# Splitting weights on ScalarE and VectorE instead of GpSimd, in a kernel of windowed attention and a GELU MLP

## The chip, the cores and the metric

The kernel runs on one core of a Trainium2 chip. The metric is the device time of one execution in microseconds (us). The engines of a core work side by side, each from its own queue in a fixed order: TensorE (PE: matrix products; PEld is its loading of stationary operands), VectorE (DVE), ScalarE (ACT), GpSimd (POOL) and SyncE (SP), which here issues DMAs. An instruction waits on semaphores for the instructions of other engines whose results or buffers it needs, and all that stands behind it in its engine's queue waits too.

## The reference

Eight batches of attention with 8 heads, 576 positions and head size 64, with a window of 128 positions back and a linear bias; the result, 4608 rows of 512, goes through an MLP with an exact GELU. All is float32.

```python
scores = scale * np.matmul(q, k.transpose(0, 1, 3, 2))
mask = (rel >= 0) & (rel < window)
scores = np.where(mask, scores + bias[None], -1000000000.0)
attn = np.exp(scores - np.max(scores, axis=-1, keepdims=True))
attn = attn / (np.sum(attn, axis=-1, keepdims=True) + 1e-09)
x = np.matmul(attn, v)            # transposed to 4608 x 512
h = x @ w_in                      # 512 x 2048, held as float64
g = 0.5 * h * (1.0 + erf(h * inv_sqrt2))
return g @ w_out                  # 2048 x 512, held as float64
```

## The kernel before

**Numbers in halves.** Most products are made in float16: an operand is scaled by a power of two, its float16 rounding is the high half, what is left is the low half, and three products (high by high, high by low, low by high) are summed. The high half is one pass of ScalarE or GpSimd, the low half one scalar_tensor_tensor of VectorE (`low_part`, line 148: in * scale - high). The scale needs the largest magnitude of the tensor: a maximum along the free axis (`absmax`, line 204), then one over the partitions (`over_partitions`, from line 109). The latter is done in one of two ways: with `early` by GpSimd's partition_all_reduce (line 113) and a floor on VectorE (114), otherwise by 13 small VectorE instructions (four copies of quarters, a reduction, a transpose, a reduction, a spread, a transpose, and four more; lines 118 to 129). `pow2` (131) and `inverse` (143) take the power of two out of the maximum by bit operations. Batches 0 to 2 use the early way (`b < 3` in `stat_v` and `split_qk`).

**Weights.** Each of w_in and w_out comes in 8 chunks of 128 x 1024 float64 words, seen as pairs of int32. `to_float32` (from line 179) makes float32 of a chunk: ScalarE takes the magnitude of the high word, read as a float (185); VectorE clamps it to two thresholds (186), shifts and masks (187), and puts in the sign and top bit (188) and three bits of the low word (191). `absmax` then finds the chunk's maximum. `split_weights` (from 195) makes the halves: ScalarE scales z in place (199) and rounds it (200), GpSimd subtracts (201). For w_in the chunks are zi, their halves wi; for w_out zo and wo. The first token tile multiplies with zo itself in float32; the later ones with wo.

**Buffers.** The raw chunks and the float32 chunks share a few slots (RAW_TAGS, Z_TAGS) with other tiles, so that a chunk can be loaded only when an earlier tenant of its slot has been read. zi 6 and 7 use the slot of zi 0 and 1 (tag ld), so ScalarE's pass on them waits until the halves of 0 and 1 are made.

**Attention.** A unit is a batch and a pair of heads: `scores` (sc, line 387, with the bias added by VectorE at 409 from the second batch on), `softmax` (maximum nmax, exponentials s on ScalarE at 450, high halves e on GpSimd at 459, or on ScalarE in batch 0, low halves on VectorE), two DMA transposes (et), and `weigh` (av, line 497), whose result ScalarE and VectorE split into x. A batch has 576 rows and a token tile 512, so that the end of a batch (tail, in batch 0) belongs to the next tile.

**MLP.** For a tile of 512 tokens, `mlp_in` (h, line 541: 16 blocks of 12 matmuls) and `mlp_out` (o, lines 576 and 579). For the first tile g is float32. For the others ScalarE makes GELU in float32 (557), GpSimd the high half (558), VectorE the low half. The product h has four PSUM banks (tag mm), shared with o; scores and av have four others (tag att).

**Order.** The program first runs batch 0's attention with w_in's conversion in between, then h of the first tile with w_out's conversion and batch 1's q, k, v, then o of the first tile with batch 1's attention and w_out's split; from then on, tile t's MLP with batch t+1's attention. The order in each queue is made by a scheduler before the run, from the program's order and priorities, and is fixed.

Of the kernel before, what the change touches and what calls it, by code (L numbers as in the profile page):

```python
# [52 lines left out]
def attention_gelu_mlp(  # L53
# [54 lines left out]

    def over_partitions(stat, n, early=False):


        if early:
            nc.gpsimd.partition_all_reduce(stat, stat, P, bass_isa.ReduceOp.max)
            nc.vector.tensor_scalar_max(stat, stat, FLOOR)
            return
# [62 lines left out]

    def to_float32(n, z):


        raw = raws.pop(n)
        lo, hi = raw[:, :, 0], raw[:, :, 1]
        zi = z.bitcast(I32)
        nc.scalar.activation(z, hi.bitcast(F32), AF.Abs)
        nc.vector.tensor_scalar(z, z, hi_thr, lo_thr, op0=ALU.min, op1=ALU.max)
        nc.vector.tensor_scalar(zi, zi, 3, 0x3FFFFFFF, op0=ALU.logical_shift_left, op1=ALU.bitwise_and)
        nc.vector.scalar_tensor_tensor(
            out=zi, in0=hi, scalar=-0x40000000, in1=zi, op0=ALU.bitwise_and, op1=ALU.bitwise_or
        )  # L190
        nc.vector.scalar_tensor_tensor(
            out=zi, in0=lo, scalar=29, in1=zi, op0=ALU.logical_shift_right, op1=ALU.bitwise_or
        )

    def split_weights(z, both, scale):

        hi = both[:, 0].rearrange("p c f -> p (c f)")
        lo = both[:, 1].rearrange("p c f -> p (c f)")
        nc.scalar.activation(z, z, AF.Copy, scale=scale)
        nc.scalar.copy(hi, z)  # L200
        nc.gpsimd.tensor_tensor(out=lo, in0=z, in1=hi, op=ALU.subtract)

# [5 lines left out]
    sww = pool.tile([P, NWP], F32, name="sww")  # L208
    pwo = pool.tile([P, NWP], F32, name="pwo")

    def weights_in(ns):

        zs = {}
        stat = small([P, len(ns)], f"stw{ns[0]}", 1)
        for n in ns:
            if n % 2 == 0:
                tag, bufs = Z_TAGS[n // 2]
                zz = pool.tile([P, 2, NW], F32, tag=tag, name=f"zi{n}", bufs=bufs)
            zs[n] = zz[:, n % 2]
            to_float32(n, zs[n])  # L220
            absmax(stat[:, n - ns[0] : n - ns[0] + 1], zs[n])
        over_partitions(stat, len(ns), True)
        r = slice(ns[0], ns[-1] + 1)
        nc.vector.tensor_scalar(pww[:, r].bitcast(I32), stat.bitcast(I32), EXPMASK, None, op0=ALU.bitwise_and)
        inverse(sww[:, r], pww[:, r])
        for n in ns:
            both = pool.tile([P, 2, NCC, 256], F16, name=f"wi{n}")
            split_weights(zs[n], both, sww[:, n : n + 1])
            wi.append(both)

    def weights_out_raw(m):

        if m % 2 == 0:
            zo.append(pool.tile([P, 2, NW], F32, tag="wo", name=f"zo{m}", bufs=4))
            zo.append(zo[m])
        to_float32(NWP + m, zo[m][:, m % 2])

    def weights_out_scale():


        for m in range(NWP):
            absmax(pwo[:, m : m + 1], zo[m][:, m % 2])
        over_partitions(pwo, NWP, True)
        nc.vector.tensor_tensor(out=pwo, in0=pwo, in1=pww, op=ALU.mult)
# [508 lines left out]
```

## Time and profile before

| what | before |
|---|---|
| median of 3 runs | 1025.76 us (1025.10 to 1026.47) |
| the profiled execution | 1023.53 us, of which span 1021.7 us |
| mean granted TensorE clock | 0.943 |
| TensorE, VectorE, ScalarE, GpSimd busy | 922.4, 653.3, 456.2, 293.9 us |
| HBM read, written | 47.32, 9.44 MB |

The span runs from the first to the last instruction of the trace. Rows of a timeline give start, duration, engine, line, operation, output<-input, count, and in square brackets the idle time ahead of it with what ended it. Rows of groups give busy time, the mean duration in ns of one, and the idle time just before them with its releasers. The parts of it that matter here are shown where they are used.

### The profile page before, as it was taken

The numbers are of one execution on the slowest core, as the hardware profiler recorded it, in microseconds if no ns is written. First come the engines' busy times: TensorE is split into PE (matmuls) and PEld (weight loads), VectorE is DVE, ScalarE is ACT, GpSimd is POOL, SyncE is SP. The second block draws the span as 40 slices with busy tenths as digits, with TensorE's granted clock in tenths as the row PEclk, the third lists the DMA queues.
The fourth block names the chain that finished last, engine by engine and source line by source line (L and its number), as shares of the span: only waits on it lengthen the run. The fifth ranks groups of instructions, "written<-read, shape, count | busy, mean of one in ns | idle before, by whom it ended". The sixth has DMA issues, their size and how long they took to land.

```text
span 1021.7 us, 17546 instructions
## 1 busy us (share of the span) xinstructions
PE 922.4 (90%) x6996; PEld 445.6 (44%) x6996; DVE 653.3 (64%) x1238; ACT 456.2 (45%) x971; POOL 293.9 (29%) x534
## 2 busy tenths in 40 slices
PE   5624998796597998999999999999999999999998
PEld 2322443343244544444445444544544444444443
DVE  5996968775397768776877787688746751201210
ACT  3755535544354446435644564356526722201200
POOL 0015020652243325411631253044314421200200
PEclk7658898797798999999999999999999999999999
DMA  9978341256124742462255234623322260000000
GB/s 286 231 170 239 110 175 66 47 114 161 47 94 83 180 110 48 93 171 63 47 104 161 62 73 89 165 66 68 84 59 47 47 125 11 1 21 21 1 11 31
DMA packets 192146, 96.69 MB, mean 95 GB/s; under 512 B 151360, under 2 KB 172864, under 8 KB 191936
## 3 DMA queue, kind: packets, MB, share of 16 engines
q1 hardware_dynamic: 187840, 87.18, 35.9%
q10 hardware_dynamic: 4224, 8.39, 2.4%
q8 instruction: 55, 0.90, 0.4%
q14 instruction: 27, 0.22, 0.1%
HBM read 47.32 MB, written 9.44 MB: 56 GB/s over the span
## 4 chain that ended last, share of the span: by engine, by line
PE 63%; DVE 17%; DMA 5%; issue 5%; ACT 5%; POOL 2%; SPq 2%; DVEq 0%; POOLq 0%; ACTq 0%
PE o L579 31%; PE h L541 21%; PE av L497 4%; PE sc L387 4%; DMA et<-e_main 3%; DMA v<-vp 2%; PE o L576 2%; DVE e_main L148 2%; DVE g L148 1%; DVE stv L204 1%; ACT s L450 1%; POOL g L558 1%; DVE stq L204 1%; SPq L293 1%; DVE stw L204 1%
## 5 line engine op out<-in xcount | busy, mean ns | idle before, releaser
L541 PE MATMUL h<-x,wi 128*128 128x512 f16 x1728 | 390.6, 385 | 24.6 <-ACT g L557 13.8
L541 PEld LDWEIGHTS <-wi 128*128 128x128 f16 x1728 | 168.0, 99 | 231.8 <-issue 37.0
L579 PE MATMUL o<-wo,g 128*128 128x512 f16 x1152 | 260.4, 380 | 3.3 <-DVE g L148 1.9
L579 PEld LDWEIGHTS <-g 128*128 128x128 f16 x1536 | 146.0, 98 | 179.2 <-DVE g L148 2.9
L558 POOL TENSOR_SCALAR g<-g,sg 128x512 f16<-128x512 f32 x128 | 106.6, 836 | 284.3 <-ACT g L557 274.7
L148 DVE SCALAR_TENSOR_TENSOR g<-g,sg,g 128x512 f16<-128x512 f32 x128 | 105.2, 834 | 95.8 <-POOL g L558 95.7
L450 ACT ACTIVATE s<-s,nmax 128x192 f32<-128x192 f32 x252 | 111.2, 442 | 102.9 <-DVE nmax L445 98.1
L557 ACT ACTIVATE g<-h,gs 128x512 f32<-128x512 f32 x128 | 86.0, 687 | 149.7 <-PE h L541 104.4
L459 POOL TENSOR_SCALAR e_main<-s,z 128x192 f16<-128x192 f32 x252 | 119.4, 492 | 109.6 <-ACT s L450 38.1
L148 DVE SCALAR_TENSOR_TENSOR e_main<-s,z,e_main 128x192 f16<-128x192 f32 x270 | 124.7, 504 | 21.4 <-POOL e_main L459 20.8
L497 PE MATMUL av<-et,vbuf 128*64 128x128 f16 (+1 forms) x1896 | 58.8, 227 | 45.3 <-DVE e L148 17.1
L387 PE MATMUL sc<-kbuf,qbuf 64*64 64x192 f16 (+1 forms) x1656 | 78.0, 273 | 22.2 <-DMA kbuf<-kp 9.3
L579 PE MATMUL o<-wo_first,g 128*128 128x512 f16 x384 | 88.9, 381 | 0.0
L497 PEld LDWEIGHTS <-vbuf 128*64 128x64 f16 x1896 | 55.1, 123 | 57.2 <-issue 36.0
L510 ACT ACTIVATE x<-av,cx 128x448 f16<-128x448 f32 (+7 forms) x56 | 26.7, 492 | 106.3 <-PE av L497 106.1
L409 DVE SCALAR_TENSOR_TENSOR s<-sc,cs,bias_h 128x384 f32<-128x384 f32 x112 | 63.8, 607 | 12.1 <-PE sc L387 11.9
L576 PE MATMUL o<-zo,g 128*128 128x512 f32 x128 | 61.1, 634 | 0.0
L445 DVE TENSOR_REDUCE nmax<-s 128x5 f32<-128x960 f32 (+1 forms) x56 | 58.6, 1046 | 3.1 <-POOL s L414 0.9
L414 POOL MEMSET s<- 64x128 f32 (+1 forms) x112 | 19.0, 171 | 136.2 <-DVE s L409 135.9
L387 PEld LDWEIGHTS <-qbuf 64*64 64x64 f16 x1512 | 37.9, 109 | 45.7 <-issue 41.7
L148 DVE SCALAR_TENSOR_TENSOR x<-av,cx,x 128x448 f16<-128x448 f32 (+7 forms) x56 | 27.9, 512 | 41.5 <-ACT x L510 41.2
L587 ACT ACTIVATE ob<-o,so 128x512 f32<-128x512 f32 x16 | 10.9, 679 | 90.3 <-PE o L579 90.2
(118 smaller groups left out, 708.0 us busy)
## 6 DMA issues: line engine op xcount, KB each, us to landing
v<-vp SPq DMA_DIRECT2D x32, 320.0 KB, 4.9
out<-ob SPq DMA_DIRECT2D x36, 256.0 KB, 2.1
raw<-w_in ACTq DMA_DIRECT2D x8, 1024.0 KB, 9.1
raw<-w_out SPq DMA_DIRECT2D x8, 1024.0 KB, 6.3
q<-qp SPq DMA_DIRECT2D x7, 1152.0 KB, 5.8
k<-kp SPq DMA_DIRECT2D x7, 1152.0 KB, 6.4
qbuf<-qp SPq DMA_DIRECT2D x4, 288.0 KB, 4.6
kbuf<-kp SPq DMA_DIRECT2D x4, 288.0 KB, 4.7
```

What stands on the lines that cost most here:

```text
L148: nc.vector.scalar_tensor_tensor(out=dst, in0=src, scalar=scale, in1=high, op0=ALU.mult, op1=ALU.subtract)
L387: nc.tensor.matmul(ps[bank][o, n, 0:W], a, m, start=(i == 0), stop=(i == len(terms) - 1 and b > 0), skip_group_check=True,)
L409: nc.vector.scalar_tensor_tensor(out=s[:, bank[0] : bank[0] + k, :], in0=ps[bank][:, 0:k, 0:W], scalar=cs, in1=bias.broadcast_to([P, k, W] ...
L445: nc.vector.tensor_reduce(out=nmax[:, r], in_=s[:, r], axis=AX.X, op=ALU.max, negate=True)
L450: nc.scalar.activation(s[:, i, :], src, AF.Exp, bias=nmax[:, i : i + 1], scale=scale, accum_out=z[:, i : i + 1])
L459: nc.gpsimd.tensor_scalar(e[:, i, 0, c], s[:, i], z[:, i : i + 1], 1.0, op0=ALU.mult, op1=ALU.mult)
L497: nc.tensor.matmul(av[r, (j - blocks[0]) * QB : (j - blocks[0] + len(js)) * QB], vbuf[:, vi, hp, kb, r], bass.AP(tensor=base.tensor, offse ...
L541: nc.tensor.matmul(ph, wi[n][:, a, cc, k * P : (k + 1) * P], x[:, cc, b, :], start=(i == 0), stop=(i == 3 * NCC - 1),)
L557: nc.scalar.activation(g32, ph, AF.Gelu, scale=gsc[t, n])
L558: nc.gpsimd.tensor_scalar(g[:, r, 0], g32, gsg[t, n], 1.0, op0=ALU.mult, op1=ALU.mult)
L576: nc.tensor.matmul(o, g[:, r, c], zo[n][:, n % 2, k * DM : (k + 1) * DM], start=(fc == 0), stop=(fc == NFC - 1))
L579: nc.tensor.matmul(o, g[:, r, a, c], wo[n][:, b, k, :], start=(fc == 0 and i == 0), stop=(fc == NFC - 1 and i == 2),)
```

## The change

It does four things. (1) `split_weights` makes the high half in one ScalarE pass, scaling and rounding at once, and the low half with `low_part` on VectorE; GpSimd has no part in it. (2) ScalarE's pass on the high words scales them by 2^-112, the upper threshold with it; the lower threshold goes, the mask after the shift goes, and the mask of the sign keeps one bit instead of two. (3) The clamp gives out its maximum over the chunk (`accum_out`), so that `absmax` on the weights goes; the maximum is now taken of words before the shift, so that its floor is another (STAT_FLOOR) and its power of two is made by a shift and a mask (`pow2_of_words`). (4) The third batch's scales for q, k and v are made by the 13 VectorE instructions (`b < 2`).

```diff
-    def over_partitions(stat, n, early=False):
+    def over_partitions(stat, n, early=False, floor=FLOOR):
         if early:
             nc.gpsimd.partition_all_reduce(stat, stat, P, bass_isa.ReduceOp.max)
-            nc.vector.tensor_scalar_max(stat, stat, FLOOR)
+            nc.vector.tensor_scalar_max(stat, stat, floor)
...
-    lo_thr = 2.0 ** -15 * 1.125
-    hi_thr = 122848.0
+    SQUEEZE = 2.0 ** -112
+    hi_thr = 122848.0 * SQUEEZE
+    STAT_FLOOR = 2.0 ** ((127 - 50) // 8 - 127) * (1 + (127 - 50) % 8 / 8)
...
-    def to_float32(n, z):
+    def to_float32(n, z, stat):
-        nc.scalar.activation(z, hi.bitcast(F32), AF.Abs)
-        nc.vector.tensor_scalar(z, z, hi_thr, lo_thr, op0=ALU.min, op1=ALU.max)
-        nc.vector.tensor_scalar(zi, zi, 3, 0x3FFFFFFF, op0=ALU.logical_shift_left, op1=ALU.bitwise_and)
+        nc.scalar.activation(z, hi.bitcast(F32), AF.Abs, scale=SQUEEZE)
+        nc.vector.tensor_scalar(z, z, hi_thr, None, op0=ALU.min, op1=ALU.max, accum_out=stat)
+        nc.vector.tensor_scalar(zi, zi, 3, None, op0=ALU.logical_shift_left)
         nc.vector.scalar_tensor_tensor(
-            out=zi, in0=hi, scalar=-0x40000000, in1=zi, op0=ALU.bitwise_and, op1=ALU.bitwise_or
+            out=zi, in0=hi, scalar=-0x80000000, in1=zi, op0=ALU.bitwise_and, op1=ALU.bitwise_or
         )
...
-        nc.scalar.activation(z, z, AF.Copy, scale=scale)
-        nc.scalar.copy(hi, z)
-        nc.gpsimd.tensor_tensor(out=lo, in0=z, in1=hi, op=ALU.subtract)
+        nc.scalar.activation(hi, z, AF.Copy, scale=scale)
+        low_part(lo, z, scale, hi)
+
+    def pow2_of_words(dst, stat):
+        nc.vector.tensor_scalar(
+            dst.bitcast(I32), stat.bitcast(I32), 3, EXPMASK, op0=ALU.logical_shift_left, op1=ALU.bitwise_and
+        )
...
-            to_float32(n, zs[n])
-            absmax(stat[:, n - ns[0] : n - ns[0] + 1], zs[n])
-        over_partitions(stat, len(ns), True)
+            to_float32(n, zs[n], stat[:, n - ns[0] : n - ns[0] + 1])
+        over_partitions(stat, len(ns), True, STAT_FLOOR)
...
-        for m in range(NWP):
-            absmax(pwo[:, m : m + 1], zo[m][:, m % 2])
-        over_partitions(pwo, NWP, True)
+        over_partitions(stwo, NWP, True, STAT_FLOOR)
+        pow2_of_words(pwo, stwo)
...
-        pwv[b], scv[b] = pow2(f"v{b}", stat, 1, 3, b < 3)
+        pwv[b], scv[b] = pow2(f"v{b}", stat, 1, 3, b < 2)
...
-        pw, sc = pow2(f"q{b}", stat, 2, 2, b < 3)
+        pw, sc = pow2(f"q{b}", stat, 2, 2, b < 2)
```

The scheduler makes another order of it. First place: GpSimd during the weights' conversion, before (stw, stv, stq are maxima of weights, v, q and k; ISA without operands is code that is put ahead of another kind of instruction):

```order
L113 ISA stw_764<-stw_764 128x2
L201 ISA
L201 TENSOR_TENSOR wi_463<-zi_446,wi_463 128x1024
...
L201 TENSOR_TENSOR wi_786<-zi_765,wi_786 128x1024
L113 ISA
L113 ISA stv_974<-stv_974 128x1
L113 ISA stw_790<-stw_790 128x2
L201 ISA
L201 TENSOR_TENSOR wi_808<-zi_791,wi_808 128x1024
L201 TENSOR_TENSOR wi_812<-zi_791,wi_812 128x1024
L113 ISA
L113 ISA stv_1088<-stv_1088 128x1
```

The same place now, up to the first e_main of batch 1 (s_0 are its scores, stwo the maxima of w_out):

```order
L113 ISA stw_757<-stw_757 128x2
L113 ISA stw_779<-stw_779 128x2
L113 ISA stv_959<-stv_959 128x1
L113 ISA stq_975<-stq_975 128x2
L422 MEMSET s_0_1200 64x128 x2
L422 MEMSET s_0_1200 64x64
L113 ISA stwo<-stwo 128x8
L467 ISA
L467 TENSOR_SCALAR e_main<-s_0_1200,z_0_1270 128x192 x5
```

The subtractions are gone with the ISA rows between them and the all-reduces; one ISA row is left, between w_out's all-reduce and batch 1's first high halves.

Second place: VectorE ahead of the last x of the first tile (x<-av_3_0, the low half that the first tile's h waits for), before:

```order
L148 SCALAR_TENSOR_TENSOR e_3_569<-s_3_471,z_3_568,e_3_569 128x192 x4
L114 TENSOR_SCALAR stw_764<-stw_764 128x2
L148 SCALAR_TENSOR_TENSOR x_379<-av_2_0_645,cx_0_249,x_379 128x512
...
L186 TENSOR_SCALAR zi_791<-zi_791 128x1024
L187 TENSOR_SCALAR zi_791<-zi_791 128x1024
L186 TENSOR_SCALAR zi_791<-zi_791 128x1024
L188 SCALAR_TENSOR_TENSOR zi_791<-raw_613,zi_791 128x1024
...
L204 TENSOR_REDUCE stv_974<-v_1_820 128x1
L191 SCALAR_TENSOR_TENSOR zi_791<-raw_613,zi_791 128x1024
L186 TENSOR_SCALAR zo_856<-zo_856 128x1024
...
L148 SCALAR_TENSOR_TENSOR x_379<-av_3_0_704,cx_0_249,x_379 128x512
```

And now:

```order
L148 SCALAR_TENSOR_TENSOR x_380<-av_2_0_638,cx_0_250,x_380 128x512
L148 SCALAR_TENSOR_TENSOR e_3_566<-s_3_468,z_3_565,e_3_566 128x192 x5
L190 TENSOR_SCALAR zi_780,stw_779<-zi_780 128x1024
L148 SCALAR_TENSOR_TENSOR e_3_566<-s_3_468,z_3_565,e_3_566 128x192 x4
...
L190 TENSOR_SCALAR zo_841,stwo<-zo_841 128x1024
L148 SCALAR_TENSOR_TENSOR wi_773<-zi_758,sww,wi_773 128x1024
L213 TENSOR_REDUCE stq_975<-q_1_886 128x1
L148 SCALAR_TENSOR_TENSOR wi_776<-zi_758,sww,wi_776 128x1024
...
L208 TENSOR_SCALAR pww<-stw_779 128x2
L148 SCALAR_TENSOR_TENSOR x_380<-av_3_0_697,cx_0_250,x_380 128x512
```

The weights' low halves (wi) stand between the last e_3 and the last x, the clamps have a second output, and the e_3 rows have moved behind x<-av_2_0.

Third place: ScalarE between batch 1's last x and the second tile's first GELUs (g_1), before:

```order
L510 ACTIVATE x_1510<-av_3_2_1997,cx_2_1100 128x128
L557 ACT_TABLE_LOAD
L557 ACTIVATE g_1_0_2072<-h_0_2058,gs_0_2052 128x512
...
L557 ACTIVATE g_1_5_2276<-h_5_2263,gs_0_2052 128x512
L344 ACTIVATE qbuf<-q_2_2033,scq_2044 128x2304
L344 ACTIVATE kbuf<-k_2_2034,scq_2044 128x2304
L557 ACTIVATE g_1_6_2293<-h_6_2280,gs_0_2052 128x512
```

And now:

```order
L518 ACTIVATE x_1504<-av_3_2_1985,cx_2_1101 128x128
L352 ACTIVATE qbuf<-q_2_2019,scq_2046 128x2304
L352 ACTIVATE kbuf<-k_2_2020,scq_2046 128x2304
L565 ACT_TABLE_LOAD
L565 ACTIVATE g_1_0_2074<-h_0_2060,gs_0_2054 128x512
L565 ACTIVATE g_1_1_2091<-h_1_2078,gs_0_2054 128x512
```

The third batch's q and k are split ahead of the first GELU instead of behind the sixth. On GpSimd, an ISA row, the all-reduce of their maxima and another ISA row stood between the first two high halves g of this tile; now nothing does.

More of the change, by code (lines that the diff above doesn't have):

```diff
@@ L157, in attention_gelu_mlp @@
     Z_TAGS = [("ld", 2), ("ld", 2), ("x", 2), ("ld", 2)]
-    lo_thr = 2.0 ** -15 * 1.125
-    hi_thr = 122848.0
+    SQUEEZE = 2.0 ** -112
+    hi_thr = 122848.0 * SQUEEZE
+    STAT_FLOOR = 2.0 ** ((127 - 50) // 8 - 127) * (1 + (127 - 50) % 8 / 8)
+    assert FLOOR == 2.0 ** -50
     NW = NCC * 256
@@ L209, in attention_gelu_mlp @@
     pwo = pool.tile([P, NWP], F32, name="pwo")
+    stwo = pool.tile([P, NWP], F32, name="stwo")
     def weights_in(ns):
@@ L219, in weights_in @@
             zs[n] = zz[:, n % 2]
-            to_float32(n, zs[n])
-            absmax(stat[:, n - ns[0] : n - ns[0] + 1], zs[n])
-        over_partitions(stat, len(ns), True)
+            to_float32(n, zs[n], stat[:, n - ns[0] : n - ns[0] + 1])
+        over_partitions(stat, len(ns), True, STAT_FLOOR)
         r = slice(ns[0], ns[-1] + 1)
-        nc.vector.tensor_scalar(pww[:, r].bitcast(I32), stat.bitcast(I32), EXPMASK, None, op0=ALU.bitwise_and)
+        pow2_of_words(pww[:, r], stat)
         inverse(sww[:, r], pww[:, r])
@@ L235, in weights_out_raw @@
             zo.append(zo[m])
-        to_float32(NWP + m, zo[m][:, m % 2])
+        to_float32(NWP + m, zo[m][:, m % 2], stwo[:, m : m + 1])
     def weights_out_scale():
-        for m in range(NWP):
-            absmax(pwo[:, m : m + 1], zo[m][:, m % 2])
-        over_partitions(pwo, NWP, True)
+        over_partitions(stwo, NWP, True, STAT_FLOOR)
+        pow2_of_words(pwo, stwo)
         nc.vector.tensor_tensor(out=pwo, in0=pwo, in1=pww, op=ALU.mult)
```

## The prediction, made before the changed kernel was timed

> **What bounds the kernel now.** I read the page's 40 slices first, then busy time by stretches, then the timeline of each engine where TensorE has gaps.
>
> ```profile
> PE 922.4 (90%) x6996; PEld 445.6 (44%) x6996; DVE 653.3 (64%) x1238; ACT 456.2 (45%) x971; POOL 293.9 (29%) x534
> ...
> PE   5624998796597998999999999999999999999998
> ...
> DVE  5996968775397768776877787688746751201210
> ...
> PEclk7658898797798999999999999999999999999999
> ```
>
> From slice 17 (about 410 us) on TensorE is full at full clock: nothing that the change touches can shorten that part, only move it. The 1021.7 - 922.4 = 99 us in which TensorE is idle, and the lower clocks, lie before it. Second view, stretches of 25 us (TensorE, its weight loads, VectorE, ScalarE, GpSimd busy; clock; DMA):
>
> ```profile
> 75.00:100.00 25.00, 13.08 (x113) 7.21 (x110) 15.04 (x11) 15.95 (x18) 13.90 (x6) 0.83 0.92 257
> 250.00:275.00 25.00, 12.73 (x54) 5.51 (x54) 9.08 (x12) 5.98 (x8) 7.24 (x7) 0.79 0.19 52
> 300.00:325.00 25.00, 19.89 (x183) 10.48 (x181) 19.07 (x59) 14.41 (x30) 9.80 (x21) 0.86 0.42 85
> ```
>
> In 75 to 100 and in 250 to 275 no engine is busy even two thirds of the time: something waits that is no work. GpSimd's own timeline says what:
>
> ```profile
> 80.50 13.90 POOL L201 TENSOR_TENSOR wi<-zi,wi 128x1024 f16<-128x1024 f32 x6 [7.08 <-ACT zi L199]
> 102.09 0.38 POOL L113 PARTITION_ALL_REDUCE stv<-stv  x1 [7.69 <-DVE zi L188]
> 140.31 0.38 POOL L113 PARTITION_ALL_REDUCE stv<-stv  x1 [8.06 <-issue]
> ...
> 251.71 2.56 POOL L558 TENSOR_SCALAR g<-g,sg 128x512 f16<-128x512 f32 x1 [14.17 <-ACT g L557]
> 262.19 0.37 POOL L113 PARTITION_ALL_REDUCE stq<-stq  x1 [7.92 <-issue]
> 270.06 2.46 POOL L558 TENSOR_SCALAR g<-g,sg 128x512 f16<-128x512 f32 x3 [7.51 <-issue]
> ```
>
> Each time GpSimd goes from arithmetic to PARTITION_ALL_REDUCE or back, 7 to 8 us pass with nothing running; the order shows a bare ISA row there. I call it a **swap**. Between 254.3 and 270.1 there are two, 7.92 + 7.51 = 15.4 us, between the first and the second half (g) that GpSimd makes of the second MLP tile's GELU.
>
> The Trainium skill, page "GPSIMD Engine Reference", section "2.1 Instruction dispatch", says that the first call of freshly loaded code pays a load of about 6 us. By that the two would be 12 us and term 4 below 3 us smaller; the rows show 7.5 to 8, and I go by them.
>
> VectorE and TensorE in the first MLP tile:
>
> ```profile
> 25.97 2.88 DVE L148 SCALAR_TENSOR_TENSOR vbuf<-v,scv,vbuf 128x2560 f16<-128x2560 f32 x1 [0.26 <-ACT vbuf L317]
> 72.79 1.40 DVE L148 SCALAR_TENSOR_TENSOR e<-s,z,e 128x192 f16<-128x192 f32 x4
> 76.50 0.75 DVE L148 SCALAR_TENSOR_TENSOR x<-av,cx,x 128x512 f16<-128x512 f32 x1 [2.23 <-ACT x L510]
> 85.92 1.44 DVE L186 TENSOR_SCALAR zi<-zi 128x1024 f32<-128x1024 f32 x1 [8.39 <-ACT zi L185]
> 92.34 3.14 DVE L188 SCALAR_TENSOR_TENSOR zi<-raw,zi 128x1024 int32<-128x1024 int32 x1
> 101.61 0.74 DVE L148 SCALAR_TENSOR_TENSOR x<-av,cx,x 128x512 f16<-128x512 f32 x1
> 140.72 0.15 DVE L114 TENSOR_SCALAR stv<-stv 128x1 f32<-128x1 f32 x1 [5.02 <-POOL stv L113]
> 167.72 1.22 DVE L204 TENSOR_REDUCE pwo<-zo 128x1 f32<-128x1024 f32 x1
> ```
>
> ```profile
> 82.89 4.32 PE L541 MATMUL h<-x,wi 128*128 128x512 f16 x18
> 90.46 4.98 PE L541 MATMUL h<-x,wi 128*128 128x512 f16 x15 [2.94 <-ACT x L510]
> 102.40 27.20 PE L541 MATMUL h<-x,wi 128*128 128x512 f16 x114 [6.96 <-DVE x L148]
> 139.93 22.48 PE L576 MATMUL o<-zo,g 128*128 128x512 f32 x52
> 166.60 1.92 PE L387 MATMUL sc<-kbuf,qbuf 64*64 64x192 f16 x30 [3.22 <-DVE kbuf L148]
> 186.55 1.17 PE L387 MATMUL sc<-kbuf,qbuf 64*64 64x192 f16 x12 [3.28 <-DVE s L409]
> 191.84 1.17 PE L387 MATMUL sc<-kbuf,qbuf 64*64 64x192 f16 x12 [2.11 <-DVE s L409]
> 192.93 16.41 PE L576 MATMUL o<-zo,g 128*128 128x512 f32 x34
> 234.68 2.77 PE L497 MATMUL av<-et,vbuf 128*64 128x128 f16 x66 [6.54 <-DMA et<-e_main]
> 251.66 10.52 PE L541 MATMUL h<-x,wi 128*128 128x512 f16 x48 [1.74 <-ACT g L557]
> 272.79 6.61 PE L541 MATMUL h<-x,wi 128*128 128x512 f16 x18 [10.61 <-ACT g L557]
> ```
>
> VectorE sets the pace of the first 140 us; TensorE waits for it and, through it, for GpSimd: 8.39 at 85.92 (ScalarE's pass into a buffer that GpSimd had not read yet, behind its swap of 7.08) and 5.02 at 140.72 (the second batch's maxima behind the swap of 8.06).
>
> **The change part by part.** Prices of one instruction:
>
> ```profile
> L201 POOL TENSOR_TENSOR wi<-zi,wi 128x1024 f16<-128x1024 f32 x8 | 18.7, 2363 | 21.7 <-ACT wi L200 14.6 <-ACT zi L199 7.1
> L204 DVE TENSOR_REDUCE stw<-zi 128x1 f32<-128x1024 f32 x8 | 9.7, 1216 | 0.0
> L191 DVE SCALAR_TENSOR_TENSOR zo<-raw,zo 128x1024 int32<-128x1024 int32 x8 | 9.8, 1222 | 0.0
> L185 ACT ACTIVATE zo<-raw 128x1024 f32<-128x1024 f32 x8 | 9.1, 1143 | 24.1 <-DMA raw<-w_out 24.1
> L199 ACT ACTIVATE zi<-zi,sww 128x1024 f32<-128x1024 f32 x8 | 8.6, 1140 | 0.0
> L186 DVE TENSOR_SCALAR zo<-zo 128x1024 f32<-128x1024 f32 x8 | 5.5, 684 | 0.0
> L129 DVE TENSOR_SCALAR stq<-back 32x2 f32<-32x2 f32 x20 | 4.4, 221 | 0.2
> L344 ACT ACTIVATE qbuf<-q,scq 128x2304 f16<-128x2304 f32 x7 | 15.4, 2205 | 0.6 <-DVE scq L143 0.6
> ```
>
> Of the 16 chunks, GpSimd loses 16 subtractions (18.7 us for the first 8), ScalarE one pass each, 16 x 1.14 = 18 us. VectorE gets 16 low parts of the form and size of L191, 1.22 each, and loses 16 maxima (L204) of 1.22: even. The 16 clamps now also accumulate. No row shows that; the ends are 0.68 (the plain clamp undisturbed, which the same work cannot undercut) and 1.22 (the reduction, which also folds a row into one number). I take 1.22, as it is the nearest in what it does: up to 16 x 0.53 = 8.5 us more on VectorE. The constants changed in the bit operations change no instruction. The third batch's two sets of scales leave GpSimd and become 13 small VectorE instructions each, at 0.22 or less (the row L129) at most 2.9 us a set. Bare ISA rows behind the first all-reduce: seven before; one is left, behind the all-reduce of w_out's maxima.
>
> *Term 1, to the end of the first tile's h (before: 139.9).* From 25.97 to 102.35 VectorE takes 76.4 us, of which 2.23 + 8.39 idle, and the four instructions from 85.92 to 95.48 (three TENSOR_SCALARs and the one at 92.34) take 9.6 us while GpSimd subtracts, against 3 x 0.68 + 1.22 = 3.3 in quiet: 6.3 lost, so 59.5 of work. In the new order 9 clamps stand ahead of the last x (9 x 0.53 = 4.8), the low parts (6) and maxima (6) cancel: about 64, and x could come at 26 + 64 = 90. But the last low part of the fourth pair's e, at 74 before (72.79 + 1.40), stands some 6 us later in the new order, and behind it come its transposes and av (TensorE's run at 82.89 began behind the first part of that av): I put x at 92 instead of 102.35. TensorE has then done 18 of the 33 early h matmuls instead of all: 15 x 0.24 us (27.20 / 114) = 3.6 to make up. **Gain 6** (0 to 12).
>
> *Term 2, the first o (140 to 222).* TensorE's waits are 3.22 for kbuf, 3.28 and 2.11 for s: VectorE's low parts of e_main stood blocked by GpSimd's subtractions. They go. New is the remaining swap ahead of e_main: VectorE's sum gives w_out's last clamp at about 150 (before, the last maximum ended at 167.72 + 1.22 = 168.9), swap done at 158, s_0's last bank at 160. TensorE needs that bank for sc_1_5, which in the new order stands behind 25 o steps of two matmuls (2 x 16.41 / 34 = 0.97 us) and the scores, at 134 + 24 + 5 = 163: covered by 3 us. Without that cover each us late costs one. **Gain 4** (-4 to 9).
>
> *Term 3, the attention tail (222 to 251.7).* The waits for transposes (6.54 the longest) shrink, since more o steps stand beside them in the new order. Against it, k_2's load is issued between et_3's two transposes, and the split of q and k of the third batch now stands ahead of the first GELU: 2 x 2.2 on ScalarE, about 5 on VectorE (two of nine tenths of the 2.88 at 25.97). **Gain 2** (-6 to 7).
>
> *Term 4, the start of the second h (251.7 to 279.4).* The two swaps go: 10.61 us idle. The 18 matmuls behind take 6.61 us instead of 18 x 10.52 / 48 = 3.9: 2.7 more. **Gain 13** (10 to 18).
>
> *Term 5, the rest.* 300 to 325 has 25 - 19.89 = 5.1 us of idle TensorE; the third batch's q and k are ready earlier, so some goes. **Gain 2** (-4 to 5).
>
> Sum 6 + 4 + 2 + 13 + 2 = 27. The profiled execution took 1023.53 (span 1021.7), the median of the three runs is 1025.76, 2.2 more. 1023.5 - 27 + 2.2 gives 998.7; I say **998**.
>
> **The rivals.** *A: more of it.* Accumulating clamps at 0.68 and a full clock in 75 to 275 (the rows above show 0.79 to 0.86): terms 1 to 3 at 11 + 8 + 6, 13 more, some 985. For it: TensorE would have fewer gaps. Against: transposes and weight loads do not get faster. *B: half of it.* The wait only moves: w_out's last load, not VectorE, sets the last clamp, it comes at 160, the swap ends at 168, and TensorE waits 8 us at sc_1_5 (term 2 at -8), with term 3 at -4: 27 - 12 - 6 = 9, or 1017. For it: ScalarE waited 24.1 us for w_out (row L185). Against: those loads wait for buffers that VectorE frees, so they come earlier as it does. *C: the change does not do what it says.* Swaps are needed for GpSimd's other arithmetic too and only move, while VectorE's new work eats terms 1 to 3: some 1025. Against it, in the order one bare ISA row is left. *D: slower.* VectorE becomes the bound through the accumulating clamp: at c us each the 16 cost 16 x (c - 0.68), and at 0.68 + (27 + 8.5) / 16 = 2.9 us the gain is used up; at 3.5, 1035. For it: VectorE's row is 9 in slices 2 and 3 already. Against: no quiet VectorE row of this size takes over 1.3 us.
>
> One more rule speaks against the third part: the Trainium skill, page "VectorE: DVE Perf Modes", section "Rules for kernel authors", sends reductions over partitions to GpSimd. By the bare instruction it is right here, 0.37 us against up to 2.9: by it the two sets cost up to 5 us and the time would be 1003. The swaps of 7.92 and 7.51 around those 0.37 decide otherwise.
>
> **How the numbers follow.** Forecast (988 to 1008) 0.58; A 0.16; B 0.17; C 0.04; D 0.05. The range runs from 982 to 1014: it takes in A but its far end and the nearer half of B, and leaves out 2 in 10. Faster by over 0.2% (about what a measurement of this kernel can tell) is everything to 1023.7: 0.91; same 0.04; slower 0.05.
>
> **What would show it.** Right: no gap of 15 us on GpSimd between its first two g halves of the second tile; one bare gap of 7 to 8 us behind the all-reduce of stwo; the clamp's row at 0.7 to 1.3 us; h's long run starting near 92; the second tile's h_4 near 232. Wrong: a clamp over 2 us, sc_1_5 waiting 8 us or more, or new gaps after 300 us.

## The result and the profile after

| | before | after |
|---|---|---|
| median, 4 runs each | 1025.43 us (1023.29 to 1026.47) | 983.13 us (980.84 to 983.70) |
| profiled execution, of which span | 1023.53, 1021.7 us | 983.70, 981.9 us |
| mean granted TensorE clock | 0.943 | 0.952 |

The ratio is 0.9586, with a 95% interval from 0.9564 to 0.9608: 42 us less. Forecast were 998 us and a range from 982 to 1014.

The page of the changed kernel: the busy line, then the 40 slices of TensorE, VectorE and the granted clock.

```profile
PE 909.1 (93%) x6996; PEld 439.3 (45%) x6996; DVE 652.4 (66%) x1279; ACT 440.2 (45%) x955; POOL 252.9 (26%) x516
...
PE   5725998967899999999999999999999999999998
...
DVE  4999997869977687768877786687557732201210
...
PEclk7656998998999999999999999999999999999999
```

TensorE is now full from slice 12 (270 us) on instead of slice 17. VectorE's busy time has hardly moved (653.3 before): the weights' low parts (20.4 us) came, the 16 maxima (19.4) went, the clamps with their second output take 6.9 us more, and other rows got shorter, the low parts of e_main by 5.8. Of the 39.8 us that the span lost, 26.5 are idle time of TensorE (1021.7 - 922.4 = 99.3 before, 981.9 - 909.1 = 72.8 now), and 13.3 are matmuls that took less time. Busy time times the share of the clock that was not granted, summed over 16 stretches of the span, gives 35 us before and 26 now: by this estimate, from clocks of two digits, some 9 of the 13.3 us are a higher granted clock.

Groups of the changed kernel (busy time, mean ns of one, idle before): VectorE's low parts, the shift and the accumulating clamp.

```profile
L148 DVE SCALAR_TENSOR_TENSOR wo<-zo,s,wo 128x1024 f16<-128x1024 f32 x8 | 10.3, 1292 | 0.0
L148 DVE SCALAR_TENSOR_TENSOR wi<-zi,sww,wi 128x1024 f16<-128x1024 f32 x8 | 10.1, 1262 | 0.0
L190 DVE TENSOR_SCALAR_CACHE_REDUCE zo<-zo 128x1024 f32<-128x1024 f32 x8 | 9.7, 1208 | 0.1
L190 DVE TENSOR_SCALAR_CACHE_REDUCE zi<-zi 128x1024 f32<-128x1024 f32 x8 | 9.6, 1204 | 0.0
```

The clamp that also folds a maximum is an operation of its own in the trace and takes 1.21 us, as long as the reduction that it replaces (1.22) and not as the plain clamp (0.68).

VectorE's last low part of the first tile's x, then TensorE's timeline, in the changed kernel:

```profile
89.17 0.73 DVE L148 SCALAR_TENSOR_TENSOR x<-av,cx,x 128x512 f16<-128x512 f32 x1
```

```profile
92.32 1.04 PE L549 MATMUL h<-x,wi 128*128 128x512 f16 x4
...
96.81 33.84 PE L549 MATMUL h<-x,wi 128*128 128x512 f16 x156
130.49 7.03 PE L584 MATMUL o<-zo,g 128*128 128x512 f32 x16
...
157.12 0.49 PE L395 MATMUL sc<-kbuf,qbuf 64*64 64x192 f16 x7 [1.91 <-DVE s L417]
158.69 1.17 PE L395 MATMUL sc<-kbuf,qbuf 64*64 64x192 f16 x17 [1.08 <-DVE s L417]
...
198.83 3.70 PE L584 MATMUL o<-zo,g 128*128 128x512 f32 x8
...
229.68 0.60 PE L395 MATMUL sc<-kbuf,qbuf 64*64 64x192 f16 x8 [4.03 <-ACT kbuf L352]
231.68 6.67 PE L549 MATMUL h<-x,wi 128*128 128x512 f16 x19 [1.40 <-ACT g L565]
...
247.44 9.45 PE L549 MATMUL h<-x,wi 128*128 128x512 f16 x43
```

The last part of x comes at 89.17 instead of 101.61; the first tile's h ends at 130.49 instead of 139.93; its o at 198.83 + 3.70 = 202.5 instead of 222.0; h_4 of the second tile starts again at 231.68 instead of 251.66. The 66 h matmuls that stood from there to 279.40 (48 and 18) are through 13 matmuls into the row at 247.44, near 250.3.

GpSimd in the changed kernel, around its one remaining swap and at the first g halves of the second tile:

```profile
146.79 0.93 POOL L113 PARTITION_ALL_REDUCE stwo<-stwo  x1 [2.28 <-DVE zo L190]
154.94 2.22 POOL L467 TENSOR_SCALAR e_main<-s,z 128x192 f16<-128x192 f32 x5 [7.22 <-issue]
...
231.72 4.00 POOL L566 TENSOR_SCALAR g<-g,sg 128x512 f16<-128x512 f32 x3 [21.76 <-ACT g L565]
```

The first three g halves run one behind the other. What GpSimd waits for there is GELU; before, two swaps of 7.92 and 7.51 us stood between them.

Last, the same stretches of the kernel before and of the changed kernel (TensorE, its weight loads, VectorE, ScalarE, GpSimd busy; clock; DMA): the first tile's o, then 200 to 300 and 300 to 470 us.

```profile
139.93:222.00 82.07, 72.64 (x448) 35.54 (x447) 64.69 (x101) 35.72 (x72) 28.19 (x40) 0.90 0.28 67
...
200.00:300.00 100.00, 76.76 (x681) 38.96 (x680) 66.17 (x105) 41.08 (x88) 39.58 (x56) 0.86 0.45 111
300.00:470.00 170.00, 161.17 (x1449) 79.68 (x1450) 128.38 (x269) 88.21 (x198) 55.57 (x121) 0.98 0.47 109
```

```profile
130.49:202.50 72.01, 69.02 (x467) 33.59 (x467) 61.89 (x120) 30.11 (x80) 17.49 (x43) 0.95 0.38 82
...
200.00:300.00 100.00, 83.09 (x732) 41.70 (x731) 80.01 (x168) 48.38 (x109) 35.29 (x68) 0.91 0.50 124
300.00:470.00 170.00, 169.86 (x1453) 82.11 (x1451) 130.08 (x262) 91.80 (x190) 57.34 (x116) 1.00 0.40 97
```

From 300 to 470 TensorE was idle for 170 - 161.17 = 8.8 us before and for 0.1 now. The prediction had given that part 2 us.

### The profile page after: what moved, and what is told of

It is laid out like the page before. It is cut to its first block, busy times and chain, and to the rows that moved or that the text cites. A ratio compares the mean times of both kernels' runs of the same rounds, so it can differ in the third digit from the quotient of the medians.

```text
span 981.9 us, 17533 instructions
## 1 busy us (share of the span) xinstructions
PE 909.1 (93%) x6996; PEld 439.3 (45%) x6996; DVE 652.4 (66%) x1279; ACT 440.2 (45%) x955; POOL 252.9 (26%) x516
## 3 DMA queue, kind: packets, MB, share of 16 engines
q10 hardware_dynamic: 4224, 8.39, 2.4%
## 4 chain that ended last, share of the span: by engine, by line
PE 72%; DVE 13%; DMA 5%; ACT 5%; issue 3%; SPq 2%; POOL 0%; ACTq 0%; DVEq 0%; POOLq 0%
PE o L587 34%; PE h L549 26%; PE av L505 5%; PE sc L395 4%; PE o L584 4%; DMA v<-vp 2%; ACT s L458 1%; DMA et<-e_main 1%; DVE e_main L148 1%; DVE stv L213 1%; DMA raw<-w_out 1%; DVE g L148 1%; DVE zi L190 1%; SPq L301 1%; ACT vbuf L325 1%
## 5 line engine op out<-in xcount | busy, mean ns | idle before, releaser
L549 PE MATMUL h<-x,wi 128*128 128x512 f16 x1728 | 386.0, 382 | 2.2 <-ACT g L565 2.0
L566 POOL TENSOR_SCALAR g<-g,sg 128x512 f16<-128x512 f32 x128 | 101.4, 795 | 287.7 <-ACT g L565 283.6
L148 DVE SCALAR_TENSOR_TENSOR g<-g,sg,g 128x512 f16<-128x512 f32 x128 | 107.7, 853 | 92.5 <-POOL g L566 92.4
L467 POOL TENSOR_SCALAR e_main<-s,z 128x192 f16<-128x192 f32 x252 | 123.1, 507 | 123.6 <-issue 43.8
L148 DVE SCALAR_TENSOR_TENSOR e_main<-s,z,e_main 128x192 f16<-128x192 f32 x270 | 118.9, 482 | 19.9 <-POOL e_main L467 19.5
L395 PE MATMUL sc<-kbuf,qbuf 64*64 64x192 f16 (+1 forms) x1656 | 73.9, 268 | 21.9 <-DMA kbuf<-kp 10.5
L395 PEld LDWEIGHTS <-qbuf 64*64 64x64 f16 x1512 | 35.7, 107 | 41.9 <-issue 38.1
L597 DVE TENSOR_SCALAR ob<-o,so 128x512 f32<-128x512 f32 x16 | 11.9, 744 | 60.0 <-PE o L587 60.0
```

The lines of the kernel that those rows point to most:

```text
L148: nc.vector.scalar_tensor_tensor(out=dst, in0=src, scalar=scale, in1=high, op0=ALU.mult, op1=ALU.subtract)
L395: nc.tensor.matmul(ps[bank][o, n, 0:W], a, m, start=(i == 0), stop=(i == len(terms) - 1 and b > 0), skip_group_check=True,)
L467: nc.gpsimd.tensor_scalar(e[:, i, 0, c], s[:, i], z[:, i : i + 1], 1.0, op0=ALU.mult, op1=ALU.mult)
L549: nc.tensor.matmul(ph, wi[n][:, a, cc, k * P : (k + 1) * P], x[:, cc, b, :], start=(i == 0), stop=(i == 3 * NCC - 1),)
L566: nc.gpsimd.tensor_scalar(g[:, r, 0], g32, gsg[t, n], 1.0, op0=ALU.mult, op1=ALU.mult)
```

## The experiments

The parts are called by their numbers in the description of the change: the first is the halves, the second and third are the scaled words with the accumulating clamp, taken together here, the fourth is the third batch's scales. Every time below is a median of 4 runs; "less" is against 7 runs of the kernel before on the same chip, "more" is against the 983.13 us above. The kernel before took 1024.3 to 1025.4 us in the four comparisons, so that a difference of about 1 us from 983.13 says nothing.

**The fourth part alone, and the change without it.**

```diff
 # the kernel before, with
-        pwv[b], scv[b] = pow2(f"v{b}", stat, 1, 3, b < 3)
+        pwv[b], scv[b] = pow2(f"v{b}", stat, 1, 3, b < 2)
...
-        pw, sc = pow2(f"q{b}", stat, 2, 2, b < 3)
+        pw, sc = pow2(f"q{b}", stat, 2, 2, b < 2)
```

> The kernel before with the fourth part alone: the third batch's scales are worked out on VectorE (b < 2 in both places), the weights stay as they were. Theory of the prediction: the two swaps of GpSimd at the start of the second h cost 13 us and nothing else changes much, so about 1011 us (1007 to 1014), with TensorE's 10.61 us gap at 272.79 gone and the 10.5 us that TensorE idled after 279 us in the kernel before still there. Rival 1: those 10.5 us after 279 belong to the same part (the third batch's q and k were late because of it); then about 1002 us and no idle TensorE after 280 us. Rival 2: the GELU's stall was covered by something else as late; then within 4 us of 1025.

998.97 us (998.21 to 1001.07), ratio 0.9753 [0.9739, 0.9768]: 26 less, double the theory, and past rival 1. What rival 1 named is there: between 300 and 470 us TensorE is idle for 0.5 us instead of 8.8. Beside that, it is idle for 9.9 us less before 200 us, where of this part only the scales of the third batch's v lie: the all-reduce at 140.31 with its swap of 8.06 is gone. TensorE in the first o of that kernel:

```profile
165.38 1.02 PE L387 MATMUL sc<-kbuf,qbuf 64*64 64x192 f16 x29 [0.25 <-DVE kbuf L148]
...
187.79 0.68 PE L387 MATMUL sc<-kbuf,qbuf 64*64 64x192 f16 x22 [0.91 <-DVE s L409]
```

The waits of 3.22, 3.28 and 2.11 us of the kernel before are 0.25, 0.43 and 0.91, though GpSimd still makes all its subtractions there. Little of this lasts: the first GELU of the second tile starts at 249.36 instead of 250.93. How much of it is the swap and how much another order was not separated.

The other way, the changed kernel with `b < 3` in both places:

> The changed kernel with the fourth part undone (b < 3 in both places). Theory: the two swaps come back at the second h and cost the 13 us of term 4, so 996 us (993 to 999). Rival 1 (the idle after 279 us belongs to this part too): 1002 to 1006. Rival 2 (with the other swaps gone the GELU's halves wait for something else): within 4 us of 983.

983.04 us (981.45 to 983.67): no loss at all. The two swaps are there. GpSimd, then TensorE, in the changed kernel without the fourth part:

```profile
221.15 0.38 POOL L113 PARTITION_ALL_REDUCE stq<-stq  x1 [9.69 <-DVE stq L213]
232.11 3.52 POOL L566 TENSOR_SCALAR g<-g,sg 128x512 f16<-128x512 f32 x3 [10.59 <-ACT g L565]
```

```profile
232.05 7.89 PE L549 MATMUL h<-x,wi 128*128 128x512 f16 x28 [0.89 <-ACT g L565]
```

The all-reduce stands ahead of the first g half, not behind it, and the swap back lies in the 10.59 us in which GpSimd waits for GELU anyhow. So rival 2 holds here, for a reason that it did not name: the first and third parts alone had already moved the split of the third batch's q and k ahead of the GELUs, and with it the swap.

**The first part alone, and the change without it.**

```diff
 # the kernel before, with
-        nc.scalar.activation(z, z, AF.Copy, scale=scale)
-        nc.scalar.copy(hi, z)
-        nc.gpsimd.tensor_tensor(out=lo, in0=z, in1=hi, op=ALU.subtract)
+        nc.scalar.activation(hi, z, AF.Copy, scale=scale)
+        low_part(lo, z, scale, hi)
```

> The kernel before with the first part alone: low parts of the weights on VectorE, one ScalarE pass, no GpSimd subtraction; masks, separate maxima and the early scales of the third batch stay. VectorE then carries 16 low parts of 1.2 us more and still all 16 maxima of 1.22. Theory: terms 1 to 3 gained 20 us in the changed kernel, of which VectorE's 16 x 0.70 (maximum and clamp apart against one accumulating clamp) is lost again, so about 1025.4 - 20 + 11 = 1016 us (1010 to 1020). Rival: VectorE is the bound of the first 220 us, so that 19 us of added work without the accumulating clamp eat the whole gain: 1025 or more.

1001.66 us (999.92 to 1002.62), ratio 0.9774 [0.9760, 0.9789]: 23.5 less, more than either theory. It is not free of swaps. GpSimd and TensorE in that kernel:

```profile
219.26 0.37 POOL L113 PARTITION_ALL_REDUCE stq<-stq  x1 [5.79 <-DVE s L408]
226.63 1.82 POOL L458 TENSOR_SCALAR e_main<-s,z 128x192 f16<-128x192 f32 x4 [7.00 <-issue]
```

```profile
233.44 2.77 PE L496 MATMUL av<-et,vbuf 128*64 128x128 f16 x66 [18.88 <-DVE e_main L148]
```

The third batch's all-reduce now splits an e_main in two, and TensorE waits 18.88 us for its other half. The swap is not all of that wait: where it is gone (first and fourth part together, below), 12.55 us remain, for the transposes.

> The changed kernel with the first part undone: the scaled word, its rounding and GpSimd's subtraction are back for the 16 chunks, clamps still accumulate and the third batch stays on VectorE. Theory: terms 1 to 3 (20 us measured) are mostly this part, less the 19 us of VectorE work that goes away with it and that was partly on the path: 983 + 14 = 997 us (992 to 1003), with three bare gaps of 7 to 8 us more on GpSimd before 160 us. Rival: the accumulating clamp alone made the gain of terms 1 to 3 and GpSimd's subtraction is free of charge: within 4 us of 983, or below.

1006.91 us (1005.20 to 1008.02): 23.8 more than the changed kernel, beyond the theory's 992 to 1003; the rival is out. Two things are undone here at once, ScalarE's pass and GpSimd's subtraction, so that they had to be told apart:

```diff
 # the changed kernel, with
-        nc.scalar.activation(hi, z, AF.Copy, scale=scale)
-        low_part(lo, z, scale, hi)
+        nc.scalar.activation(z, z, AF.Copy, scale=scale)
+        nc.scalar.copy(hi, z)
+        nc.vector.tensor_tensor(out=lo, in0=z, in1=hi, op=ALU.subtract)
```

> The changed kernel with ScalarE's extra pass back and GpSimd still out: the words are scaled in place, rounded in a second pass, and VectorE subtracts; 16 x 1.14 = 18 us more on ScalarE. It tells apart what the first part gains by ScalarE from what it gains by GpSimd. Theory (the prediction cost ScalarE's pass at nothing): 984 us (981 to 988), so the 24 us between this kernel and the one with GpSimd's subtraction, 1006.9, are GpSimd's. Rival (ScalarE is on the path between scale and half): 992 or more.

987.50 us (986.96 to 988.94): 4.4 more than the changed kernel, at the upper edge of the theory. The program at 1006.91 differs from this one in the engine of that subtraction alone. So of the 23.8 us, 19.4 come with GpSimd and 4.4 with ScalarE's pass, which the prediction had cost at nothing, each with the order that it brings (both have the late split). GpSimd's timeline in the kernel with the subtraction, up to the second batch:

```profile
61.54 12.70 POOL L205 TENSOR_TENSOR wi<-zi,wi 128x1024 f16<-128x1024 f32 x4 [6.88 <-ACT wi L204]
81.03 3.38 POOL L205 TENSOR_TENSOR wi<-zi,wi 128x1024 f16<-128x1024 f32 x1 [6.79 <-ACT wi L204]
90.60 0.37 POOL L113 PARTITION_ALL_REDUCE stw<-stw  x1 [6.18 <-DVE zi L191]
99.19 4.20 POOL L205 TENSOR_TENSOR wi<-zi,wi 128x1024 f16<-128x1024 f32 x2 [8.21 <-ACT wi L204]
113.02 0.38 POOL L113 PARTITION_ALL_REDUCE stv<-stv  x1 [9.63 <-issue]
120.54 2.58 POOL L205 TENSOR_TENSOR wi<-zi,wi 128x1024 f16<-128x1024 f32 x1 [7.14 <-ACT g L563]
```

Each turn from subtraction to all-reduce or back is a gap of 6 to 10 us; some of these gaps also hold a wait for another engine. The gap of 6.79 us ahead of 81.03 is no turn: it lies between two subtractions and ends with ScalarE's rounding.

**The third part alone, and the change without it.** The third part alone is the kernel before with the new `to_float32` and `pow2_of_words`; the change without it is the kernel before with the edits of the first and the fourth part above.

> The kernel before with the third part alone: scaled words, no masks, the accumulating clamp; GpSimd subtracts, and the third batch's scales stay on GpSimd, with the swap now between the fifth and sixth g half of the second tile. Theory: VectorE's 11 us are worth little while GpSimd's subtractions and their swaps set the pace, and the swap among the g halves still costs 13: 1020 us (1014 to 1026). Rival (VectorE is the bound by itself): 1025.2 - 11 = 1014 or less.

1005.09 us (1002.53 to 1007.53), ratio 0.9809 [0.9770, 0.9847]: 20 less, well past the theory. The rival's bound (1014 or less) holds it, but not its sum: VectorE's 11 us do not make 20. The all-reduce stands behind the fifth g half there. GpSimd, then TensorE, in that kernel:

```profile
251.37 0.37 POOL L113 PARTITION_ALL_REDUCE stq<-stq  x1 [7.12 <-DVE g L148]
258.74 2.46 POOL L567 TENSOR_SCALAR g<-g,sg 128x512 f16<-128x512 f32 x3 [7.00 <-issue]
```

```profile
266.83 0.37 PE L396 MATMUL sc<-kbuf,qbuf 64*64 64x192 f16 x4 [7.25 <-ACT kbuf L353]
```

TensorE loses 7.25 us there, at the scores, not 10.61 at h.

> The changed kernel with the third part undone: masks and the 16 separate maxima are back (16 x (0.68 + 1.22 - 1.20) = 11 us more on VectorE), halves on VectorE and the third batch's scales on VectorE stay. In the kernel with the first part alone a swap stood between the two halves of e_main (7.00 us of GpSimd at 226.63) and TensorE waited 18.9 us there. Theory (a swap costs what stands behind it at its place): that wait goes with the fourth part, 1001.7 - 9 to 13 = 990 us (987 to 994), and the maxima are the 7 that remain against 983. Rival (the parts add up, each by its own): 1001.7 - 26.2 = 975.5 us.

992.73 us (992.00 to 993.49), in the theory's range: 9.6 more than the changed kernel, where 16 x (0.68 + 1.22 - 1.20) = 11 us of work had been put back on VectorE. The rival, that the parts add up, is far out. TensorE in that kernel, at the end of the first tile's h and in the attention tail:

```profile
128.82 25.05 PE L575 MATMUL o<-zo,g 128*128 128x512 f32 x58
...
223.97 2.77 PE L496 MATMUL av<-et,vbuf 128*64 128x128 f16 x66 [12.55 <-DMA et<-e_main]
```

The first tile's h ends at 128.82, ahead of the 130.49 of the changed kernel, although VectorE has more to do. The loss lies behind it: the second tile's first GELU starts at 242.54, against 230.94.

All eight combinations:

| first (halves) | third (clamp) | fourth (scales) | us | less than before |
|---|---|---|---|---|
| - | - | - | 1025.4 | |
| yes | - | - | 1001.7 | 23.5 |
| - | yes | - | 1005.1 | 20.3 |
| - | - | yes | 999.0 | 26.2 |
| yes | yes | - | 983.0 | 42.1 |
| yes | - | yes | 992.7 | 32.7 |
| - | yes | yes | 1006.9 | 18.3 |
| yes | yes | yes | 983.1 | 42.3 |

The three alone sum to 70 us, together they give 42. Without the first part the third adds nothing to the fourth (999.0 becomes 1006.9); on top of the other two the fourth adds nothing.

**What a swap costs, by itself.**

```diff
 # the changed kernel, in mlp_in, behind the high half of g
+        if t == 1 and fc == 0:
+            extra = small([P, 2], "extra", 1)
+            nc.vector.tensor_copy(extra, g32[:, 0:2])
+            nc.gpsimd.partition_all_reduce(extra, extra, P, bass_isa.ReduceOp.max)
```

> The changed kernel with one all-reduce of a 128x2 copy added behind the third g half of the second tile; nobody reads its result, and the order of ScalarE and of TensorE's h stays. So GpSimd makes two swaps more (7 to 8 us each) in the place where the kernel before had them. Theory: TensorE stands still there as it did before (10.61 us, and slower matmuls behind): 983.1 + 13 = 996 us (993 to 1001), and so the first kernel's loss there was the swap itself, wherever it came from. Rival (the gap of before was that of the late split of q and k, not of the swap): within 4 us of 983.

993.10 us (990.88 to 995.10): 10.0 more. GpSimd, then TensorE, in that kernel:

```profile
240.74 0.37 POOL L570 PARTITION_ALL_REDUCE extra<-extra  x1 [7.27 <-issue]
248.18 2.46 POOL L566 TENSOR_SCALAR g<-g,sg 128x512 f16<-128x512 f32 x3 [7.07 <-issue]
```

```profile
254.43 1.17 PE L395 MATMUL sc<-kbuf,qbuf 64*64 64x192 f16 x12 [9.93 <-DVE s L417]
```

Two swaps, 14.3 us of GpSimd, and TensorE stands 9.93 us behind VectorE, whose low part of g waits for GpSimd. The theory holds: the loss is the swap's. ScalarE's order in that kernel is that of the changed kernel, GpSimd's has only the all-reduce more, and VectorE's differs by the copy and a few small instructions. In the fifth tile (`t == 4 and fc == 4`):

> The changed kernel with the same unread all-reduce of a 128x2 copy, now in the fifth tile, where TensorE is at work all the time: it shows whether the 10.0 us that one cost in the second tile are the price of a swap among g halves or of that place. Theory: VectorE's low part of g waits for GpSimd's half, the scores' evictions are queued behind it, and TensorE waits for them as it did (9.93 us): 993 us (988 to 996). Rival (in the steady tiles three g buffers and four PSUM banks cover 14 us of GpSimd): within 2 us of 983.

990.75 us (989.25 to 990.99): 7.6 more, in the theory's range. The profiled execution, at 989.25, is 5.6 us above that of the changed kernel, and TensorE waits once, for 5.44 us and not 9.93, in a stretch where the changed kernel does not wait:

```profile
560.93 2.77 PE L505 MATMUL av<-et,vbuf 128*64 128x128 f16 x66 [5.44 <-DVE s L417]
```

**What a late split costs.** The eight kernels of the table fall in two kinds: in five the third batch's q and k are split ahead of the GELUs, and TensorE is idle up to 0.6 us between 300 and 470 us; in three (none, third alone, third and fourth) the split is late, and TensorE is idle for 5.9 to 8.8 us. So that lateness looked like the missing term.

```diff
 # the changed kernel, with split_qk(2) moved to step 1 of the second tile, and
+        if gate is not None:
+            nc.vector.tensor_copy(stat[:, 0:1], gate)
...
+                    split_qk(2, g_of[1, 0][:, 0, 0, 0:1])
```

> The changed kernel with the split of q and k of the third batch held back: a copy of one number of the first g half of the second tile is put ahead of its maxima, so that it cannot start before that g is there; its scales stay on VectorE and no swap is added. Theory (the lateness of this split has a price of its own): third tile's attention is pushed on, the third tile takes some 104 us between its last o and that of the tile before, as in the kernel before (463.8 - 359.9), instead of 97, and the time is 990 us (986 to 994). Rival (only swaps cost, a late split is hidden behind h): 983 us, within 3.

984.13 us (982.36 to 985.31): the rival. The split is late (TensorE's scores at 248.28 wait for kbuf instead of those at 229.68), and the stretch from 300 to 470 loses what it lost before, but 200 to 300 wins as much:

```profile
200.00:300.00 100.00, 91.78 (x738) 45.82 (x738) 77.26 (x159) 36.96 (x88) 32.47 (x63) 0.97 0.46 117
300.00:470.00 170.00, 161.31 (x1441) 79.85 (x1436) 129.88 (x263) 91.21 (x191) 57.04 (x115) 0.97 0.41 99
```

Idle: 8.2 and 8.7 us, against 16.9 and 0.1 in the changed kernel. The attention that is not done beside the second tile is done beside the third, and that is all.

> The same, with the third batch's scales on GpSimd again (b < 3), so that an all-reduce and two swaps stand behind the sixth g half of the second tile, as in the kernel before they stood behind the first. Theory (lateness and swap each have a price): 983 + 7 + 10 = 1000 us (995 to 1006), against 983.0 where the same all-reduce stood ahead of the g halves. Rival (the swap hides the lateness or the reverse): 993 or less.

983.15 us (982.15 to 987.26): a swap among the g halves, behind the sixth, for nothing. GpSimd waits 5.82 and 7.05 us around the all-reduce and TensorE 7.15 us at the scores, but at the transposes behind them it waits 6.2 us less than the kernel without the swap (1.95 + 2.02 against 4.13 + 6.01):

```profile
245.63 1.40 PE L397 MATMUL sc<-kbuf,qbuf 64*64 64x192 f16 x16 [7.15 <-ACT kbuf L354]
...
281.41 1.55 PE L507 MATMUL av<-et,vbuf 128*64 128x128 f16 x54 [1.95 <-DMA et<-e_main]
...
327.40 1.55 PE L507 MATMUL av<-et,vbuf 128*64 128x128 f16 x54 [2.02 <-DMA et<-e_main]
```

```profile
279.21 2.77 PE L507 MATMUL av<-et,vbuf 128*64 128x128 f16 x54 [4.13 <-DMA et<-e_main]
...
326.76 2.77 PE L507 MATMUL av<-et,vbuf 128*64 128x128 f16 x54 [6.01 <-DMA et<-e_main]
```

The first fence is the late split with the swap, the second the one without. Here TensorE has waits of its own a little later, and the swap ahead of them costs nothing.

**The last swap off the path.**

```diff
 # the changed kernel, with
-            nc.vector.tensor_scalar_max(stat[k * QP : (k + 1) * QP, 0:n], back[:, 0:n], FLOOR)
+            nc.vector.tensor_scalar_max(stat[k * QP : (k + 1) * QP, 0:n], back[:, 0:n], floor)
...
-        over_partitions(stwo, NWP, True, STAT_FLOOR)
+        over_partitions(stwo, NWP, False, STAT_FLOOR)
```

> The changed kernel with the maxima of w_out reduced over partitions on VectorE instead of GpSimd: 13 small instructions, at most 2.9 us, ahead of the first e_main, and the all-reduce of 0.93 us and the gap of 7.22 us behind it are no longer between the last clamp and e_main. Theory: TensorE's 1.91 + 1.08 us of waiting at sc_1_5 go: 980 us (978 to 982). Rival (the swap only moves, since GpSimd still has to load its arithmetic ahead of the first e_main, and the wait was VectorE's own): within 1.5 us of 983, or slower.

983.14 us (982.00 to 983.89): no gain. The 3.0 us at sc_1_5 are gone, and 3.6 us of waits stand 25 us later; TensorE in that kernel:

```profile
157.37 0.69 PE L395 MATMUL sc<-kbuf,qbuf 64*64 64x192 f16 x24
...
181.10 0.53 PE L395 MATMUL sc<-kbuf,qbuf 64*64 64x192 f16 x8 [2.47 <-DVE x L148]
...
183.72 2.77 PE L505 MATMUL av<-et,vbuf 128*64 128x128 f16 x66 [1.15 <-DMA et<-e_main]
```

No experiment beats the changed kernel by more than 0.1 us; four of them lie within 1 us of it.

## Why the prediction was right, and where it was not

The range held the time and the sign was right; the forecast (998; its sum gives 998.7) was 15 us too slow. The likeliest case's own range, from 988, did not hold it, and the range reached down to 982 only because it took in rival A. So it is in part luck that it held.

**Term 1, gain 6 (0 to 12): 9.4** (139.93 - 130.49). The mechanism was right. The clamp was taken at 1.22 us and is 1.21. x was done at 89.90 (89.17 + 0.73), 2 us ahead of the 92 forecast; dense h runs from 92.32. What gave this gain is the first part: h ends at 131.74 with the first part alone and at 142.12 with the fourth alone. VectorE's total load did not decide it: with the 16 maxima back on VectorE, h ended at 128.82. What counts is what the order puts ahead of the last x, 6 maxima and 4 low parts in that kernel, 9 accumulating clamps and 6 low parts in the changed one, and that VectorE's wait of 8.39 us and the slow rows beside GpSimd's subtractions are gone.

**Term 2, gain 4 (-4 to 9): 10** (222.0 - 202.5 = 19.5, less the 9.4). This term was mis-sized, and left its range. The waits went from 9.4 us (82.07 - 72.64) to 3.0, by 6.4. The other 3.6 are TensorE's busy time, 72.64 to 69.02: at the granted clocks in the same two rows, 72.64 x 0.90 = 65.4 and 69.02 x 0.95 = 65.6, which fits nearly the same work (the 128 o matmuls are in both) at a higher clock. The sum had no such term outside rival A. The cover at sc_1_5 was put at 3 us and was 3 us short; rival B, with 8, did not come. Taking that wait away gave nothing, so it was no loss of the end time either. The reason given for the old waits, VectorE blocked by GpSimd's subtractions, is not borne out: with the fourth part alone the subtractions stay, and the waits nearly go, though in another order. The all-reduce at 140.31, behind whose swap VectorE waited 5.02 us, was taken for the second batch's; it is that of the third batch's v, and goes with the fourth part.

**Term 3, gain 2 (-6 to 7): 0.5**, and h_4 at 231.68 where 232 was forecast.

**Term 4, gain 13 (10 to 18): some 9** (279.40 - 250.3 = 29.1, less the 20.0 to h_4). That is just under its range; two swaps put back among the g halves cost 10.0. But its step that "the two swaps go" because the scales leave GpSimd failed as a reason: with the scales on GpSimd the changed kernel is as fast. What took the swaps off the path is the new place of the split, ahead of the first GELU, which term 3 had read in the order and booked only as a cost. The fourth part is worth 26 us alone and 0 beside the others.

**Term 5, gain 2 (-4 to 5): 10.7** (39.8 - 29.1), the largest miss. Of it 6.5 us are idle time of TensorE, 15.0 us behind 279.40 before and 8.5 behind 250.3 now: the forecast took "some" of the 5.1 us that it had found in one stretch; there were 8.8 between 300 and 470, and all went, but a wait of 3.9 at 270.40 came. The other 4.2 are busy time, of which some 2.5 is work already done: 54 of the third batch's scores stand ahead of 250.3 in the changed kernel. The reason given, that q and k are ready earlier, fits every kernel's split and idle time; but the experiment that makes only the split late shows that this alone moves idle time from one tile to the next and changes the end by 1 to 2 us. So the idle time before 300 and that behind it have to be counted together. That swap, late split and late attention added up in the kernel before, and that each part alone broke this up in another way, fits the table but is not shown: no run holds the order fixed.

**Rival A** named 985, through clamps at 0.68 and a full clock. The clamps were not at 0.68, and the granted clock in 75 to 275 rose from 0.86 to 0.90 only. So the number came out by other means. **C** is half true: one of four parts does nothing beside the others. **D** needed a clamp of 2.9 us. The swaps of the added all-reduce (7.27 and 7.07 us) are near the rows that the prediction went by. The Trainium skill, page "GPSIMD Engine Reference", section "2.1 Instruction dispatch", has about 6 for a load of code; the measured gaps decide. The change took 983.14 us with one more reduction over partitions on VectorE, and 983.04 with the third batch's on GpSimd. So the rule that sends them to GpSimd (the Trainium skill, page "VectorE: DVE Perf Modes", section "Rules for kernel authors") decided nothing here; where the prediction says that it speaks against the third part, it means the fourth.

What stays open: some 4 of the 13.3 us less of TensorE's busy time, which the granted clocks do not account for; why the third part makes 8 us of loss on top of the fourth when GpSimd subtracts, which was not followed further than to its other order; and, for every part, what is its own and what is the order that the scheduler made with it.

## What to carry to other kernels

A swap on GpSimd has no price of its own: two of 6 to 7 us cost 10.0, 7.6 and 0 us at three places. In the first two VectorE's half waited behind them and TensorE behind VectorE; in the third TensorE had other waits soon after. Where a scheduler makes the order, read the new order first, and ask of each part what it is worth beside the others: the part that gained 26 us alone gained nothing beside the others, and leaving one part out of the whole told what adding it alone did not. Idle time saved in one stretch is a gain only when the next stretch does not have it instead: with the late split 8.7 us went from one to the next.

## What the hardware showed beside this

A VectorE clamp of 128x1024 float32 with an accumulated maximum takes 1.20 to 1.21 us, against 0.68 without, and 0.08 us more for reading the accumulator. GpSimd's subtraction on 128x1024 took 2.86 us on average for w_in and 2.14 for w_out in the changed kernel without the first part; VectorE's took 1.22. And the mean granted clock did not order the runs of one kernel: of the four of the fourth part alone, the one at 0.981 took 1001.07 us and those at 0.949 to 0.954 took 998.21 to 999.12. In the profile of the run at 1001.07 the clock of the first 100 us is 0.98, against 0.71 in the kernel before, and TensorE waits there for 45 us of 100; the other three left no profile.
